# One granule's x transposed on SyncE's DMA queue instead of TensorE, its FFN half moved, and two granules' loads released later

## The chip, the cores and the metric

The kernel runs on one core of a Trainium2 chip. The metric is the device time of one execution in microseconds. Of the 47 executions of the kernel before that were timed beside the experiments, 46 lie within 0.3% of their median, 208.63 us (one took 209.83). "PE" is TensorE, "DVE" VectorE, "ACT" ScalarE, "POOL" GpSimd, "SP" SyncE. The profile's span is about 1.8 us shorter than the device time of the same execution (207.4 against 209.15 before, 212.9 against 214.69 changed).

## The reference

```python
# attention: q, k, v are (4 batches, 8 heads, 768 positions, 64), float32
scores = q @ k.T / sqrt(64) + bias(head, distance)
keep   = (key position < 8) | (0 <= row - column < 96)
x = (softmax(where(keep, scores, -1e9)) @ v)      # -> (3072 tokens, 512)
# feed-forward (FFN), with w_in (512, 2048), w_out (2048, 512)
h = x @ w_in
out = (s * relu(h)**2 + b) @ w_out                # (3072, 512) float32
```

## The kernel before

The 3072 tokens are handled as 12 granules of 256 tokens (numbers 0 to 11; three per batch). A granule passes through five stations:

1. GpSimd issues six loads (k, q and v of two blocks of 128 rows), cast to bfloat16 on the way.
2. k and q are transposed, by PE for granules 0 to 3, by four DMA transposes on SyncE's queue for the others.
3. PE makes scores, ACT the exponentials, DVE the masks, PE the product with v, DVE the normalised result `xn`.
4. `xn` is transposed to `xT`, by PE for granules 0 to 3 and by two DMA transposes on SyncE's queue for the others.
5. PE multiplies with `w_in` in eight pieces of 8 matmuls each (the first FFN half, 1.75 us for two pieces), ACT and DVE square, PE multiplies with `w_out`.

Loads are held back by a tiny copy on GpSimd that reads one element of something; everything behind it on the queue waits until that element is there (in the kernel before the gate of granule 8 waited 11.86 us, and the first load behind it was issued at 83.87 us, 0.40 us after it).

```python
X_PE, LEAD = 4, 4

def x_by_dma(j):
    t = xT_tile(j)
    for i in range(GB):                                    # two blocks
        nc.sync.dma_start_transpose(t[:, :, i * P : (i + 1) * P], xn[j][:, i, :])

def hold_loads(ap):                                        # the gate
    g = work.tile([P, 1], BF16, name="gate", tag="gate")
    nc.gpsimd.tensor_copy(g[0:1, :], ap)

def finish_granule(j):
    if j < X_PE:
        x_by_pe(j)
    else:
        x_by_dma(j)
    if 6 <= j + LEAD < NJ:                                 # loads of granule j + 4
        hold_loads(xT[j][0:1, 0, GT - 1 : GT])
        load_granule(j + LEAD)

def step(s, c0, c1, c2, pool=None, pre=()):                # half a granule, from granule 4 on
    j = 2 * s // HP
    last = (2 * s + 2) % HP == 0
    if not last and j >= 4 and j + 2 < NJ:
        qk_by_dma(j + 2)                                   # SyncE: k, q of granule j + 2
    posts = scores(s + 1)
    # ... exponentials, masks, c0, product with v, c1, product with v, c2 ...
    if last:
        finish_granule(j)
    # ...

# ... granules 0 to 3 by hand ...
finish_granule(3)
run(scores(8))
# ...
step(8, [lambda: rest(2, 0)] + late_p1(3, (0,)), late_p1(3, (1, 2)), late_p1(3, (3,)))
step(9, p2[2][1:2], late_p1(3, (4, 5)), late_p1(3, (6, 7)))
```

`late_p1(3, ...)` are pieces of the first FFN half of granule 3; `rest(2, ...)` and `p2[2]` are the output product of granule 2. SyncE's queue carries, in program order, the transposes of k and q, the transposes of x and the output stores. A transpose whose source has not landed stops all that is behind it (in the changed kernel's trace the queue stood 5.5 us for one k load of granule 6). "Landing" is the time when a transfer's data have arrived; where a landing time of two transposes is given, it counts from the issue of the second.

The softmax here doesn't subtract the row's maximum and nothing guards it: scores larger than these inputs give would overflow.

## Time and profile before

The median was 208.58 us in three runs (208.42 to 208.96).

| Reading | Before |
|---|---|
| PE busy | 202.1 of 207.4 us |
| longest wait of PE after the start | 0.51 us, for q of granule 5 |
| DMA engines | busy nearly without a pause from 40 to 79 us |
| PE transposes of granule 3's x | 0.54 us of PE time |

From the page of the kernel before: the span, the busy times, and two of the rows that cut the span into 40 slices (busy share in tenths).

```profile
span 207.4 us, 5323 instructions
...
PE 202.1 (97%) x2191; PEld 160.1 (77%) x2191; DVE 161.3 (78%) x338; ACT 128.5 (62%) x198; POOL 68.9 (33%) x90
...
PE   7999999999999999999999999999999999999993
...
DMA  5999999999999999999999999999570300240006
```

PE is busy all the time, so only PE work removed, or a wait of PE removed, can shorten the kernel. The DMA row: until about 140 us the DMA engines have hardly a free moment.

From PE's timeline of the kernel before (start, length, instruction group; in brackets the idle time before it and what ended it): the transposes that the change removes, the next scores, the one wait, scores, and the first FFN half of granule 5.

```profile
58.52 0.61 PE L591 MATMUL ps_x<-ident_bf,xn 128*128 128x128 bf16 x8
59.06 0.45 PE L441 MATMUL ps_s<-qx,kx 64*128 64x128 bf16 x8
...
69.10 0.34 PE L441 MATMUL ps_s<-qx,kx 64*128 64x128 bf16 x6 [0.51 <-DMA qx<-nat]
...
94.12 0.62 PE L441 MATMUL ps_s<-qx,kx 64*128 64x128 bf16 x16
...
98.35 1.91 PE L619 MATMUL ps<-xT,w_in_bf 128*128 128x256 bf16 x16
```

From POOL's timeline of the kernel before: the gates before the loads of granules 6, 7, 8 and 9.

```profile
51.16 0.18 POOL L122 COPY gate<-xT 1x1 bf16<-1x1 bf16 x1
...
61.62 0.18 POOL L122 COPY gate<-xT 1x1 bf16<-1x1 bf16 x1
...
83.29 0.18 POOL L122 COPY gate<-xT 1x1 bf16<-1x1 bf16 x1 [11.86 <-DMA xT<-xn]
...
97.71 0.18 POOL L122 COPY gate<-xT 1x1 bf16<-1x1 bf16 x1 [8.60 <-DMA xT<-xn]
```

From the DMA view of the kernel before, short windows around 60.2 and 91.2 us (last number: us from issue to landing): the last q transpose of granule 5 and the x of granule 5.

```profile
qx<-nat SPq DMA_TRANSPOSE x1, 8.9
...
xT<-xn SPq DMA_TRANSPOSE x2, 6.4
```

The x of granule 5 was issued at 89.92 and 91.23, and landed at 97.59. PE used it at 98.35.

### The profile page before, as it was taken

The numbers are of one execution on the slowest core, as the hardware profiler recorded it, in microseconds if no ns is written. First come the engines' busy times: TensorE is split into PE (matmuls) and PEld (weight loads), VectorE is DVE, ScalarE is ACT, GpSimd is POOL, SyncE is SP. The second block draws the span as 40 slices with busy tenths as digits, with TensorE's granted clock in tenths as the row PEclk, the third lists the DMA queues.
The fourth block names the chain that finished last, engine by engine and source line by source line (L and its number), as shares of the span: only waits on it lengthen the run. The fifth ranks groups of instructions, "written<-read, shape, count | busy, mean of one in ns | idle before, by whom it ended". The sixth has DMA issues, their size and how long they took to land.

```text
span 207.4 us, 5323 instructions
## 1 busy us (share of the span) xinstructions
PE 202.1 (97%) x2191; PEld 160.1 (77%) x2191; DVE 161.3 (78%) x338; ACT 128.5 (62%) x198; POOL 68.9 (33%) x90
## 2 busy tenths in 40 slices
PE   7999999999999999999999999999999999999993
PEld 2678884557867485878888898888888889888883
DVE  7786599977989856799799974699866696737974
ACT  5875669486976548786664595663695764476200
POOL 8985333799365300810900828200000000000000
PEclk9999999999999999999999999999999999999999
DMA  5999999999999999999999999999570300240006
GB/s 164 172 179 202 207 206 177 155 152 129 110 150 120 151 132 218 155 213 212 152 198 153 125 154 178 194 172 126 52 206 0 95 14 0 56 150 0 0 9 196
DMA packets 110836, 28.17 MB, mean 136 GB/s; under 512 B 97852, under 2 KB 109308, under 8 KB 110812
## 3 DMA queue, kind: packets, MB, share of 16 engines
q0 software_dynamic: 76000, 13.11, 90.1%
q1 hardware_dynamic: 33612, 14.13, 41.7%
q10 hardware_dynamic: 1200, 0.59, 1.1%
q8 instruction: 17, 0.28, 0.6%
q14 instruction: 7, 0.06, 0.1%
HBM read 27.26 MB, written 6.29 MB: 162 GB/s over the span
## 4 chain that ended last, share of the span: by engine, by line
PE 65%; DMA 23%; POOL 9%; issue 1%; DVE 0%; POOLq 0%
PE ps L619 29%; PE ps L819 24%; DMA nat<-in_q_dram 12%; DMA w_in_bf<-in_moe_w_in_dram 6%; PE ps L667 5%; DMA qx<-nat 4%; PE ps_s L441 4%; PE ps_av L495 3%; POOL vb L108 3%; POOL nat L102 3%; POOL w_in_bf L140 2%; POOL nat L116 1%; PE ps_last L819 0%; DVE o_last L828 0%; POOL rel L173 0%
## 5 line engine op out<-in xcount | busy, mean ns | idle before, releaser
L619 PE MATMUL ps<-xT,w_in_bf 128*128 128x256 bf16 x768 | 90.3, 273 | 0.0
L629 ACT ACTIVATE gT<-ps 128x512 bf16<-128x512 f32 x96 | 55.8, 599 | 46.8 <-PE ps L619 46.6
L619 PEld LDWEIGHTS <-w_in_bf 128*128 128x128 bf16 x768 | 73.0, 98 | 9.4 <-DVE xT L594 0.2
L450 ACT ACTIVATE pt<-ps_s 128x1024 bf16<-128x1024 f32 (+1 forms) x44 | 39.3, 946 | 3.3 <-PE ps_s L441 3.3
L667 PE MATMUL ps<-w_out_bf,gT 128*128 128x512 bf16 x128 | 29.7, 380 | 0.0
L457 DVE TENSOR_TENSOR pt<-pt,tmpl 128x1024 bf16<-128x1024 bf16 (+1 forms) x40 | 24.6, 645 | 3.8 <-ACT pt L450 3.7
L819 PEld LDWEIGHTS <-gsum 128*128 128x128 bf16 x256 | 24.1, 98 | 3.7 <-DVE gsum L782 0.5
L108 POOL DMA_DIRECT2D vb<-in_v_dram x24 | 21.4, 906 | 6.9 <-DMA w_out_bf<-in_moe_w_out_dram 3.4
L793 DVE TENSOR_TENSOR gT<-gT 128x1024 bf16<-128x1024 bf16 x20 | 13.7, 686 | 11.7 <-ACT gT L629 11.7
L667 PEld LDWEIGHTS <-gT 128*128 128x128 bf16 x128 | 11.7, 98 | 13.0
L466 DVE TENSOR_TENSOR xn<-ps_av,rc 128x256 bf16<-128x256 f32 x48 | 20.4, 425 | 1.7
L819 PEld LDWEIGHTS <-gT 128*128 128x128 bf16 x200 | 18.6, 98 | 2.3
L465 DVE RECIPROCAL rc<-ps_av 128x4 f32<-128x4 f32 x48 | 8.6, 179 | 12.3 <-PE ps_av L495 10.4
L116 POOL DMA_DIRECT2D nat<-in_k_dram x16 | 14.2, 885 | 9.2 <-DMA nat<-in_k_dram 5.1
L495 PEld LDWEIGHTS <-pt 128*128 128x128 bf16 x320 | 14.4, 97 | 2.7 <-DVE xn L466 0.7
L632 DVE TENSOR_TENSOR gT<-gT 128x512 bf16<-128x512 bf16 x32 | 13.0, 422 | 3.5 <-ACT gT L629 3.3
L495 PE MATMUL ps_av<-vb,pt 128*128 128x65 bf16 x208 | 15.5, 193 | 0.0
L819 PE MATMUL ps<-w_out_bf,gsum 128*128 128x256 bf16 x128 | 15.3, 273 | 0.0
L116 POOL DMA_DIRECT2D nat<-in_q_dram x16 | 14.2, 888 | 2.9 <-DMA w_in_bf<-in_moe_w_in_dram 1.9
L819 PE MATMUL ps<-wsub,gsum 128*128 128x256 bf16 x128 | 15.1, 273 | 0.0
L819 PE MATMUL ps<-w_out_bf,gT 128*128 128x256 bf16 x120 | 13.9, 273 | 0.0
L122 POOL COPY gate<-xT 1x1 bf16<-1x1 bf16 x6 | 1.1, 176 | 35.9 <-DMA xT<-xn 35.9
(112 smaller groups left out, 228.5 us busy)
## 6 DMA issues: line engine op xcount, KB each, us to landing
out_dram<-o_q SPq DMA_DIRECT2D x15, 256.0 KB, 2.6
vb<-in_v_dram POOLq DMA_DIRECT2D x24, 128.0 KB, 8.3
nat<-in_k_dram POOLq DMA_DIRECT2D x22, 128.0 KB, 7.7
nat<-in_q_dram POOLq DMA_DIRECT2D x22, 128.0 KB, 7.6
w_out_bf<-in_moe_w_out_dram POOLq DMA_DIRECT2D x4, 512.0 KB, 16.2
w_in_bf<-in_moe_w_in_dram POOLq DMA_DIRECT2D x4, 256.0 KB, 7.4
w_in_bf<-in_moe_w_in_dram POOLq DMA_DIRECT2D x2, 512.0 KB, 11.3
out_dram<-o_sb SPq DMA_DIRECT2D x4, 256.0 KB, 6.3
```

Source lines behind the costliest of these rows:

```text
L108: nc.gpsimd.dma_start(vbuf[b % 2][:, sb, :, 0:D], rows_of(v, b, sb))
L116: nc.gpsimd.dma_start(t[:, n, i, :, :], rows_of(srcs[n], b, sb))
L450: nc.scalar.activation(pt[:, :, 0:ncol], ps[:, :, 0:ncol], ACT.Exp, scale=QSCALE)
L457: nc.vector.tensor_tensor(pv, pv, m.rearrange("p h a c -> p h (a c)"), ALU.mult)
L466: nc.vector.tensor_tensor(dst, av[:, :, :, 0:D], rc[:].to_broadcast((P, 2, 2, D)), ALU.mult)
L495: nc.tensor.matmul(av[:, i, hi, 0 : D + 1], lhsT=pt[:, hi, c * P : (c + 1) * P], rhs=vv, start=(n == 0), stop=(n == len(terms) - 1),)
L619: nc.tensor.matmul(ps[:, i, :], lhsT=w_in_bf[:, kc, fc * P : (fc + 1) * P], rhs=xT[j][:, kc, :], start=(kc == 0), stop=(kc == KC - 1),)
L629: nc.scalar.activation(gs, ps[:], ACT.Relu)
L632: nc.vector.tensor_tensor(gs, gs, gs, ALU.mult)
L667: nc.tensor.matmul(po[:], lhsT=g_of(j)[:, fc, tb * P : (tb + 1) * P], rhs=w_out_bf[:, fc, :], start=(fc == 0), stop=(fc == FC - 1),)
L793: outs.append(lambda: nc.vector.tensor_tensor(gs, gs, gs, ALU.mult))
L819: nc.tensor.matmul(ps[:, tb, cs], lhsT=stat[:, fc, tb * P : (tb + 1) * P], rhs=mov[:, fc, cs], start=(fc == 0), stop=(fc == NH - 1),)
```

## The change

The intent: take granule 3's eight transposes and two copies off PE, DVE and ACT; give its x time to arrive by putting granule 2's output product first; and keep loads out of the way of the transposes, by releasing granule 6's loads when granule 3's x has landed and granule 7's when the q transposes of granule 6 have landed.

```diff
-    X_PE = 4
+    X_PE = 3
...
-        if 6 <= j + LEAD < NJ:
+        if 8 <= j + LEAD < NJ:
             hold_loads(xT[j][0:1, 0, GT - 1 : GT])
             load_granule(j + LEAD)
...
             qk_by_dma(j + 2)
+            if j == 4:
+                hold_loads(qk_of(2, 1)[0:1, 1, HP - 1, P - 1 : P])
+                load_granule(7)
...
     finish_granule(3)
+    hold_loads(xT[3][0:1, 0, GT - 1 : GT])
+    load_granule(6)
...
-    step(8, [lambda: rest(2, 0)] + late_p1(3, (0,)), late_p1(3, (1, 2)), late_p1(3, (3,)))
-    step(9, p2[2][1:2], late_p1(3, (4, 5)), late_p1(3, (6, 7)))
+    step(8, [lambda: rest(2, 0)], [lambda: p2_mm(2, 1, 0, FC // 2)], [lambda: rest(2, 1)])
+    step(9, late_p1(3, (0, 1, 2)), late_p1(3, (3, 4)), late_p1(3, (5, 6, 7)))
```

## The prediction

> **What bounds the kernel now.** PE. The page gives it 202.1 of 207.4 us busy, at a granted clock of 0.998. After the start its timeline shows one wait over 0.2 us: 0.51 us at 68.6, the scores of granule 5, "<-DMA qx<-nat". So the change can gain only removed PE work plus that wait, and loses any new PE wait.
>
> From 40 to 79 us the DMA engines hardly rest (stretches: DMA share 1.7 to 2.8). Transposes and loads slow each other: those of granule 5 took 8.4 to 8.9 us from issue to landing (the last 60.19 to 69.06), against 2.4 to 2.5 us with no load in flight (147 us, 163 us). [...]
>
> **What changes.** Gone: eight PE transposes of x (58.52 to 59.06, 0.54 us of PE), a 0.42 us DVE and a 0.58 us ACT copy. Added: two DMA transposes (1.2 to 1.3 us of SyncE's issue each). Moved: four FFN pieces of granule 3 behind granule 2's output; loads of granules 6 and 7 start later.
>
> **Critical path.**
> 1. The 0.54 us is mostly not kept there: granule 4's last transpose lands at 59.12, its scores start at 59.06 now. From 58.5 PE would wait about 0.5 us.
> 2. Granule 5's loads are queued before granule 6's, so still land at about 60.2; its transposes then run nearly alone and land at 64 to 66, not 69: the 0.51 us wait goes. Granule 3's x, issued behind them at 61.7 to 64.3, lands at 66 to 68; PE wants it at about 68.8. Thin margin, no wait.
> 3. Granule 6's loads start at about 67.5 instead of 51.3, 7's at about 80 instead of 61.7: a serial chain of loads (first landing 4.2 us, six issues 5.3 us), transposes, loads, transposes, 12 to 13 us a round. Granule 6 is ready at 79 to 81 (wanted 81.2), 7 at 92.5 to 95 (wanted 93.6).
> 4. Granule 7's transposes, waiting for loads until about 89, head SyncE's queue before output stores and granule 5's x. That x, now issued at 89.92 and landed at 97.59, would land at 99 to 100; PE wants it at 98. I expect 0.5 to 1.5 us of new PE wait there or at granule 7's scores.
>
> Sum: 208.58 - 0.5 + about 0.7 = 208.8 us, 80% range 207.7 to 210.6. Faster by over 2%: 0.01 (there are not 4 us to take). Within 2%: 0.95. Slower by over 2%: 0.04.
>
> **What would show each step.** PE's timeline: a wait near 58.6 for granule 4's qx, none near 68.5; granule 5's transposes landing in 4 to 6 us; GpSimd's gate copies at 66 to 68 and 79 to 81; PE waits for "qx<-nat" near 94 or "xT<-xn" near 98; PE busy down about 0.5 us.
>
> **What would make it wrong.** If rounds take 10 us, step 4's waits vanish: 207.9 to 208.1. If 15 us, waits of 2 to 4 us appear at granules 6 and 7: 211 to 213. If granule 5's loads land earlier, everything after shifts earlier. PE could wait for PSUM where all eight FFN pieces of granule 3 now stand together (ACT 0.60 us each beside two exponentials of 0.97, against PE's 0.87 each); I expect it not to.

## The result

The changed kernel took 215.28 us (median of four runs, 214.69 to 216.16) against 208.50 (208.34 to 208.96). The ratio is 1.0325, 95% interval 1.0285 to 1.0365. Ratios here are the mean time of one kernel's fast runs over that of the other's fast runs of the same rounds, so they are not quite the ratio of the medians. On this one core a run is called slow when it is over 1.5% above the fastest run of the same kernel; the medians below are over all runs.

From the page of the changed kernel:

```profile
span 212.9 us, 5299 instructions
...
PE 202.5 (95%) x2175; PEld 160.4 (75%) x2183; DVE 161.2 (76%) x337; ACT 127.9 (60%) x197; POOL 69.9 (33%) x90
...
PE   6999999999999999975899999999999999999993
...
DMA  5999999999996999999999999994161210240005
```

PE's row has a hole that was not there before, in the slices 18 to 20 counted from the left (90 to 106 us). In the DMA row the first breath comes in slice 13, at 64 to 69 us, where the held loads had only just been released (65.14 us) and had not landed.

From PE's timeline of the changed kernel:

```profile
58.77 0.40 PE L441 MATMUL ps_s<-qx,kx 64*128 64x128 bf16 x8
...
93.20 0.23 PE L441 MATMUL ps_s<-qx,kx 64*128 64x128 bf16 x2
94.53 0.57 PE L441 MATMUL ps_s<-qx,kx 64*128 64x128 bf16 x14 [1.10 <-DMA qx<-nat]
...
102.00 2.73 PE L619 MATMUL ps<-xT,w_in_bf 128*128 128x256 bf16 x16 [3.12 <-DMA xT<-xn]
104.87 2.63 PE L619 MATMUL ps<-xT,w_in_bf 128*128 128x256 bf16 x16
```

Up to 93 us the change works. The first wait is gone, and PE starts the scores of granule 7 at 93.20 instead of 94.12, 0.92 us earlier. Then PE waits 1.10 us for the q of granule 7 and 3.12 us for the x of granule 5. After that the same 16 matmuls take 2.73 and 2.63 us that took 1.91 before.

From POOL's timeline of the changed kernel, the gates before the loads of granules 6, 7, 8 and 9:

```profile
65.14 0.18 POOL L122 COPY gate<-xT 1x1 bf16<-1x1 bf16 x1 [14.10 <-DMA xT<-xn]
...
78.19 0.40 POOL L122 COPY gate<-qx 1x1 bf16<-1x1 bf16 x1 [7.32 <-DMA qx<-nat]
...
83.90 0.32 POOL L122 COPY gate<-xT 1x1 bf16<-1x1 bf16 x1
...
102.08 0.18 POOL L122 COPY gate<-xT 1x1 bf16<-1x1 bf16 x1 [12.66 <-DMA xT<-xn]
```

Granule 6's loads start 14 us later than before, granule 7's 16.6 us later, granule 8's 0.6 us later. So the loads of 7 and 8, whose issues had 12.4 us of rest between them (71.4 to 83.9), now follow each other without a pause from 78.7 to 89.4 us. The last load of granule 8 landed at 97.13 before and lands at 104.43 now.

From the DMA view of the changed kernel, short windows around 59.5, 62.6 and 92.6 us: the last q transpose of granule 5, the x of granule 3, the x of granule 5.

```profile
qx<-nat SPq DMA_TRANSPOSE x1, 4.6
...
xT<-xn SPq DMA_TRANSPOSE x2, 2.5
...
xT<-xn SPq DMA_TRANSPOSE x2, 9.3
```

The q transpose, beside the last packets of granule 5's loads, lands in 4.6 us, and the x of granule 3, with no load packet from 62.5 to 65.1 us, in 2.5: the late release does what it was meant to do there. But the x of granule 5, issued at 91.35 and 92.62, lands at 101.95.

From the table by stretches of the changed kernel (busy us of each engine, then the granted clock, DMA share and GB/s):

```profile
core 0: us, PE busy (x) PEld busy (x) DVE busy (x) ACT busy (x) POOL busy (x), PEclk, DMA share, GB/s
102.00:104.00 2.00, 2.00 (x14) 1.61 (x15) 0.00 (x0) 0.60 (x1) 1.50 (x3) 0.74 1.30 233
104.00:106.00 2.00, 2.00 (x16) 1.49 (x15) 0.87 (x3) 0.60 (x1) 2.00 (x3) 0.50 1.54 223
```

The clock record of the trace has 0.5 from 102.94 on for 3.41 us. Half a clock for 3.41 us costs 1.7 us (an estimate). The same stretches of the kernel before ran at 1.00.

The balance of the two profiled spans: 0.92 us gained by 93 us, then 1.10 + 3.12 of waits and 1.7 of half clock lost; that makes +5.0, and the spans differ by 212.9 - 207.4 = 5.5 us. About half a microsecond is not put down to anything. The profiled execution of the changed kernel was its fastest; the other three had clocks of 0.983 to 0.991.

### The profile page after: what moved, and what is told of

The parts are those of the page before. It is cut to its first block, busy times and chain, and to the rows that moved or that the text cites. A ratio compares the mean times of both kernels' runs of the same rounds, so it can differ in the third digit from the quotient of the medians.

```text
span 212.9 us, 5299 instructions
## 1 busy us (share of the span) xinstructions
PE 202.5 (95%) x2175; PEld 160.4 (75%) x2183; DVE 161.2 (76%) x337; ACT 127.9 (60%) x197; POOL 69.9 (33%) x90
## 4 chain that ended last, share of the span: by engine, by line
PE 89%; DMA 7%; ACT 1%; issue 0%; SPq 0%; ACTq 0%; DVE 0%
PE ps L619 40%; PE ps L819 21%; PE ps L667 13%; PE ps_s L441 5%; PE ps_av L495 5%; DMA xT<-xn 4%; DMA first<-in_q_dram 3%; PE ps_t L351 1%; PE ps_s L517 1%; PE ps_s L532 1%; PE ps_av L558 1%; PE ps_x L591 0%; PE ps_t L341 0%; PE ps_last L819 0%; SPq L599 0%
## 5 line engine op out<-in xcount | busy, mean ns | idle before, releaser
L619 PE MATMUL ps<-xT,w_in_bf 128*128 128x256 bf16 x768 | 91.5, 275 | 3.2 <-DMA xT<-xn 3.1
L667 PE MATMUL ps<-w_out_bf,gT 128*128 128x512 bf16 x120 | 28.7, 379 | 0.5 <-issue 0.2
L793 DVE TENSOR_TENSOR gT<-gT 128x1024 bf16<-128x1024 bf16 x20 | 13.7, 686 | 12.4 <-ACT gT L629 12.4
```

The source lines that it names most:

```text
L619: nc.tensor.matmul(ps[:, i, :], lhsT=w_in_bf[:, kc, fc * P : (fc + 1) * P], rhs=xT[j][:, kc, :], start=(kc == 0), stop=(kc == KC - 1),)
L667: nc.tensor.matmul(po[:], lhsT=g_of(j)[:, fc, tb * P : (tb + 1) * P], rhs=w_out_bf[:, fc, :], start=(fc == 0), stop=(fc == FC - 1),)
L793: outs.append(lambda: nc.vector.tensor_tensor(gs, gs, gs, ALU.mult))
```

## The experiments

Theory A: granule 7's loads come late, so its transposes block SyncE's queue late; granule 5's x is issued late behind them and shares the DMA engines with granule 8's loads; PE waits, and the idle time brings the half clock. Rival B: the loss comes of granule 3's x on SyncE's queue, or of PE's new order. All kernels below gave correct results. "Before" was run again beside each batch (medians 208.54 to 208.90).

| Run | Median us | Ratio to before (95%) | PE waits over 0.5 us after 60 us, in its profile |
|---|---|---|---|
| changed kernel | 215.28 | 1.0325 (1.0285 to 1.0365) | 1.10 (q of 7), 3.12 (x of 5) |
| late_loads | 213.57 | 1.024 (1.0193 to 1.0286) | 2.95 (x of 5) |
| queue_order | 211.41 | 1.0133 (1.0097 to 1.0169) | 2.45 (x of 3) |
| order_only | 208.86 | 1.0007 (0.9993 to 1.002) | none |
| x5_pe | 210.66 | 1.0095 (1.006 to 1.0131) | 0.96 (q of 7), 0.99 (x of 6) |
| busy_wait | 213.46 | 1.0257 (1.0195 to 1.0319) | 1.40 (q of 7) |
| hold8 | 212.94 | 1.0177 (1.0117 to 1.0237) | 1.31 (x of 5), 1.24 (q of 8) |
| pool_stores | 211.60 | 1.0127 (1.0104 to 1.015) | 2.69 (q of 7) |
| defer | 212.97 | 1.0229 (1.017 to 1.0287) | 2.08 (q of 7) |
| hold8_act | 214.30 | 1.0248 (1.0209 to 1.0287) | 1.92 and 2.75 (ACT) |
| hold8_defer | 217.12 | 1.0386 (1.0332 to 1.044) | 1.67 and 3.88 (q of 8) |
| seven_free | 213.30 | 1.0212 (1.0189 to 1.0236) | 1.09 (q of 6), 2.27 (x of 4) |
| seven_nat6 | 216.40 | 1.0186 (1.0162 to 1.021), two fast runs | 3.62 (x of 4) |
| seven_nat6_x4 | 213.40 | no interval, one fast run | 2.67 (x of 5) |
| queue_six_nat5 | 209.30 | 1.0033 (1.0019 to 1.0048) | 0.83 (x of 3) |
| split5 | 210.57 | 1.0096 (1.0063 to 1.0129) | 2.13 (q of 5) |
| six_nat5, six_nat5b | 208.68, 208.78 | 0.9996 (0.9983 to 1.001), one run | none |

### Which part of the change loses: late_loads, queue_order, order_only

late_loads is the kernel before with only the gates moved. As granule 3's x is made by PE there, the first gate reads the last q transpose of granule 5, which opens at nearly the same time (64.26 against 65.14 us).

```diff
# late_loads, against the kernel before
-        if 6 <= j + LEAD < NJ:
+        if 8 <= j + LEAD < NJ:
...
+            if j == 4:
+                hold_loads(qk_of(2, 1)[0:1, 1, HP - 1, P - 1 : P])
+                load_granule(7)
...
     finish_granule(3)
+    hold_loads(qk_of(1, 1)[0:1, 5, HP - 1, P - 1 : P])
+    load_granule(6)
```

> The kernel before with only the loads moved: granule 6's released by the landed q transposes of granule 5, granule 7's by the landed q transposes of granule 6; granule 3's x stays on PE and PE's order is the old one. Theory A (the loss is the serial chain of late loads: granule 7's transposes late, granule 5's x late, PE waits, clock drops): gates open at about 64 and 77 us, PE waits for qx near 94 and for xT near 98 as in the changed kernel, time 212 to 215. Rival B (the loss comes of granule 3's x on SyncE's queue or of the new PE order): 208 to 209, no wait over 1 us near 98.

PE's timeline of late_loads near 100 us:

```profile
100.99 3.55 PE L619 MATMUL ps<-xT,w_in_bf 128*128 128x256 bf16 x16 [2.95 <-DMA xT<-xn]
```

213.57 us: the late loads alone cost 4.8 of the 6.8 us, with the wait for granule 5's x at the same place, and a stretch of 3.41 us at half clock behind it (100.95 us on). The other wait that was expected, for a q near 94, did not come. Rival B cannot explain this, as granule 3's x is on PE and PE's order is the old one. Theory A is only half right, though. The DMA view of late_loads, a window around 91.2 us, has for granule 5's x:

```profile
xT<-xn SPq DMA_TRANSPOSE x2, 9.7
```

Its two transposes were issued at 89.99 and 91.27 here, as in the kernel before (89.92 and 91.23), and landed at 100.94 instead of 97.59. So here nothing was issued late, and the whole delay lies between issue and landing.

queue_order is the complement: the changed kernel with the old gates. order_only also sets `X_PE` back to 4.

```diff
# queue_order, against the changed kernel (order_only: and X_PE = 4)
-        if 8 <= j + LEAD < NJ:
+        if 6 <= j + LEAD < NJ:
...
-            if j == 4:
-                hold_loads(qk_of(2, 1)[0:1, 1, HP - 1, P - 1 : P])
-                load_granule(7)
...
-    hold_loads(xT[3][0:1, 0, GT - 1 : GT])
-    load_granule(6)
```

> The changed kernel with the loads of granules 6 and 7 released as in the kernel before (granule 2's x, granule 3's x): the queue and order part of the change alone. Theory A (the late loads carry the loss): granule 3's x and the q transposes of granule 5 share the DMA engines with granule 6's loads again and land at about 69 and 71, PE waits 1.5 to 3 us near 69, no wait near 94 or 98, time 208.5 to 210.5. Rival B (queue and order carry the loss): 213 or more.

PE's timeline of queue_order near 70 us:

```profile
71.69 4.15 PE L619 MATMUL ps<-xT,w_in_bf 128*128 128x256 bf16 x24 [2.45 <-DMA xT<-xn]
```

Here granule 3's x shares the DMA engines with granule 6's loads, takes 8.8 us to land, and PE waits 2.45 us. This may be why the change moved the gates at all. The time, 211.41, is above the 208.5 to 210.5 that was expected; the wait lies in the range expected, and two of six runs (213.1 us) had a clock of 0.991 and 0.992; the profiled one of the two had the half clock.

> The kernel before with only PE's new order (granule 2's output ahead of all eight FFN pieces of granule 3), x of granule 3 on PE, loads as before. Theory A: nothing changes, 208 to 208.9, the wait of about 0.5 us for the q transposes of granule 5 near 68 stays. Rival B2 (eight FFN pieces in one step wait for PSUM): 1 us or more longer, with waits of PE between 69 and 77.

208.86 us against 208.90: PE's new order costs nothing, and eight FFN pieces in a row do not run out of PSUM here (no PE wait over 0.5 us after 60 us in its profile). The wait of 0.5 us that I expected to stay was not in its profile.

### The half clock: busy_wait

28 matmuls that nobody reads were put before the FFN piece that waits.

```diff
# busy_wait, against the changed kernel (step 13)
+    def fill(n, w=2 * P):
+        ps = ps_h.tile([P, w], F32, name="ps_w", tag="psh")
+        for _ in range(n):
+            nc.tensor.matmul(ps[:], lhsT=ones_bf[:], rhs=w_out_bf[:, 0, 0:w], start=True, stop=True)
...
-            [u1(o, 0)],
+            [lambda: fill(28)] * (pr == 2) + [u1(o, 0)],
```

> The changed kernel with 28 matmuls of 256 columns that nobody reads (about 3.05 us) put before the FFN piece that waits for granule 5's x, so that PE works through the wait. If the half-clock stretch is caused by the idle time, it vanishes and the time falls by 1.4 to 1.7 us to about 213.5, with the FFN piece starting at the same time. If the clock drop has another cause, the time stays at 215.

PE's timeline and the table by stretches of busy_wait:

```profile
98.84 3.22 PE L1169 MATMUL ps_w<-w_out_bf,ones_bf 128*128 128x256 bf16 x28
101.99 1.91 PE L619 MATMUL ps<-xT,w_in_bf 128*128 128x256 bf16 x16
...
102.00:106.00 4.00, 4.00 (x49) 3.44 (x50) 1.21 (x3) 1.93 (x4) 3.58 (x5) 1.00 1.44 222
```

The FFN piece starts at 101.99, as in the changed kernel (102.00), but its 16 matmuls take 1.91 us and the clock is 1.00. The median falls to 213.46, as expected. Here doing nothing useful is faster than waiting: the half clock is a consequence of the idle time, and it makes a wait of 3.1 us cost 4.8 (an estimate: 3.1 + 1.7). The medians fall by 1.8 us and the profiled spans by 1.6 (212.9 to 211.3); the intervals of the two ratios overlap a little, and one run of four still took 216.05 us at a clock of 0.992, so the size rests on the profile, the cause on both.

The clock records say more (worked out from them and from PE's timelines). In the changed kernel's record 98.99 us at full clock is 29 times 3.413 us, then come 3.41 at half, then 105.81 at full clock, 31 times; in the record of the kernel before the 201.39 us at full clock are 59 times. So in these two records the clock changes at whole steps of 3.413 us. The idle time of PE within the 3.41 us that end where a half clock begins was 1.85 us in queue_order, 2.08 in defer, 2.47 in the changed kernel, 2.56 in pool_stores, 2.62 in hold8_act, 2.67 in seven_nat6_x4, 2.92 in late_loads and 3.18 in hold8_defer. A longer wait of 3.62 us in seven_nat6 was followed by no half clock, nor was one of 2.27 in seven_free or one of 2.13 in split5. Steps of 3.413 us cut these waits into 1.93 and 1.69, 0.94 and 1.33, 1.02 and 1.11 (an estimate from the clock records and the PE timelines). So the length of a wait does not settle alone whether a half clock follows. That it matters where among the steps a wait falls is my reading of these numbers; no run moves a wait along them to test this, and 1.85 us within one step was followed by a half clock while 1.93 was not.

### What makes granule 5's x late: x5_pe, hold8, pool_stores, defer, hold8_act, hold8_defer

```diff
# x5_pe, against the changed kernel
-        if j < X_PE:
+        if j < X_PE or j == 5:
             x_by_pe(j)
```

> The changed kernel with granule 5's x transposed by PE. Theory A with the clock drop as a second-order loss: the wait of 3.1 us for xT and the stretch of 3.4 us at half clock vanish, 0.54 us of PE work comes back, the wait of 1.1 us for qx stays: 5.5 - 3.1 - 1.7 + 0.5 = 1 to 1.5 us over before in the span, 209.5 to 211. Rival C (granule 5's x is only the first thing that is late, the next ones stop PE as long): over 213.

210.66 us. The wait and the half clock went, the wait for granule 7's q stayed, as theory A has it. PE's timeline of x5_pe holds one more wait than expected:

```profile
95.48 0.57 PE L441 MATMUL ps_s<-qx,kx 64*128 64x128 bf16 x14 [0.96 <-DMA qx<-nat]
...
117.53 1.92 PE L619 MATMUL ps<-xT,w_in_bf 128*128 128x256 bf16 x16 [0.99 <-DMA xT<-xn]
```

With granule 5's x out of the way, granule 6's x is the next that comes late.

hold8 moves granule 8's loads away from granule 5's x.

```diff
# hold8, against the changed kernel
-        if 8 <= j + LEAD < NJ:
+        if 9 <= j + LEAD < NJ:
...
                 load_granule(7)
+            if j == 5:
+                hold_loads(qk_of(2, 1)[0:1, 3, HP - 1, P - 1 : P])
+                load_granule(8)
```

> The changed kernel with granule 8's loads released by the landed q transposes of granule 7 instead of granule 4's x. Theory A1 (granule 5's x is late because granule 8's loads share the DMA engines with it; in the changed kernel its transposes took 9.3 us from issue to landing against 6.4 before): it lands in 4 to 6 us, at about 97, waits near 94 and 98 shrink to under 0.5 us together, time 207.5 to 209. Theory A2 (it is late because it is issued late, behind granule 7's transposes on SyncE's queue): issue stays at 91.4, landing at 99 or later, wait over 1 us, time over 210. Granule 8 itself may come late near 108.

PE's timeline of hold8:

```profile
98.75 1.92 PE L619 MATMUL ps<-xT,w_in_bf 128*128 128x256 bf16 x16 [1.31 <-DMA xT<-xn]
...
110.54 0.57 PE L441 MATMUL ps_s<-qx,kx 64*128 64x128 bf16 x14 [1.24 <-DMA qx<-nat]
```

From POOL's timeline of hold8, the gate and the first load behind it:

```profile
91.74 0.18 POOL L122 COPY gate<-qx 1x1 bf16<-1x1 bf16 x1 [8.05 <-DMA qx<-nat]
92.31 0.88 POOL L116 DMA_DIRECT2D nat<-in_k_dram  x1 [0.40 <-DMA out_dram<-o_sb]
```

The x, issued at 90.82 and 92.45, landed 6.2 us after issue instead of 9.3, at 98.7. The gate opened while its transposes were being issued, and packets of the loads run from 94 us on, so hold8 delays the sharing with granule 8's loads and does not take it away: the 3 us are a part of what the sharing costs. I had expected 97 and waits under 0.5 us together; x still came 1.3 us late, and granule 8's q now came late too. 212.94 us, with a wide spread (211.1 to 213.8 in fast runs).

The rest is the place in SyncE's queue, behind output stores. In the changed kernel the last input of granule 5's x was ready at 87.8 us. Its transposes were issued at 91.35, because granule 7's transposes (until 88.8) and four of the five output stores stood ahead. pool_stores issues the five stores from GpSimd; defer issues them on SyncE behind the x.

```diff
# pool_stores (defer: the same five, appended to a list that is issued after x_by_dma(5))
-        nc.sync.dma_start(out[t0 : t0 + P, :], o_sb[:])
+        nc.gpsimd.dma_start(out[t0 : t0 + P, :], o_sb[:])
```

> The changed kernel with five output stores (granule 3's first block, the four early ones) issued from GpSimd instead of SyncE, so that granule 5's x is not behind them: in the changed kernel its last input was ready at 87.8 and its transposes were issued at 91.35. Head of line theory: issue at 88.9 (after granule 7's transposes), landing at 97 to 99.5, the wait at x falls from 3.1 to under 1.5 us, the half clock goes, time 210 to 212. Contention theory: issued earlier but landing not before 101, time stays at 214 to 216.

> The changed kernel with the same five output stores issued on SyncE after granule 5's x instead of before it. Head of line alone: x issued at 88.9 to 90.5 instead of 91.35, landing at 97.5 to 100 beside granule 8's loads, wait at x 0.5 to 2 us (changed kernel 3.1), the wait of 1.1 us at granule 7's q stays; 210.5 to 213.

PE's timeline of pool_stores (first line) and of defer (second line):

```profile
96.45 0.93 PE L441 MATMUL ps_s<-qx,kx 64*128 64x128 bf16 x14 [2.69 <-DMA qx<-nat]
...
96.11 0.67 PE L441 MATMUL ps_s<-qx,kx 64*128 64x128 bf16 x14 [2.08 <-DMA qx<-nat]
```

In both the x's first transpose was issued about 1.3 us earlier, at 89.99 and 90.11. The second landed 7.7 and 7.5 us after its own issue instead of 9.3, at 99.03 and 98.85. So of the 3 us gained, less than half is the earlier issue; the rest is a shorter time from issue to landing, as the four stores of 256 KB no longer stand in front. (In the changed kernel's trace SyncE's queue moves the stores' packets of 2 KB from 94 to 97 us, before the x's packets of 256 bytes.) PE no longer waited for the x of granule 5, beyond a short wait at 83 us (0.34 and 0.39 us) that is granule 4's. But in the same runs the wait for granule 7's q grew from 1.10 to 2.69 and 2.08 us, and the half clock, which was expected to go, followed that wait instead (3.41 us from 96.32 and from 96.44). 211.60 and 212.97 us: both in their expected range, though not by the split of waits that I expected.

hold8_act and hold8_defer move both the stores and granule 8's loads away from the x.

> hold8 with the five output stores issued from ScalarE, so that granule 5's x is neither behind them on SyncE's queue nor beside granule 8's loads. If these two together are why it is late: issued at about 89, landing at 94 to 96, PE waits for no x near 98 (hold8: 1.3 us, changed kernel: 3.1 us), half clock gone. What is left is granule 8 itself (1.2 us near 110 in hold8): time 208.5 to 210.5. If a wait over 1 us at x stays, a third cause is at work.

This one is spoilt. The x's first transpose landed after 4.0 us and no wait for x was left, but ScalarE now stood still at the stores: it had been idle for 3.69 us before 82.32 us, with a store issued at 81.89 (the trace names DVE as what it waited for), and for 3.42 us before 94.00, with two stores issued from 92.63 on (the trace names a q transpose). PE waited 1.92 and 2.75 us for ACT. Its time says nothing about the theory.

> Both taken away without ScalarE's queue, which spoilt hold8_act: granule 8's loads held until granule 7's q has landed, and the five stores behind granule 5's x on SyncE. If these two are the whole cause of the late x: it lands at 93.5 to 96, no wait at 98 and none at granule 7's q, no half clock; left is a wait of 1 to 2 us for granule 8's q near 110: 208.5 to 210.5.

From the DMA view of hold8_defer, a window around 90.3 us, and from its PE timeline:

```profile
xT<-xn SPq DMA_TRANSPOSE x1, 2.5
```

```profile
109.67 0.23 PE L441 MATMUL ps_s<-qx,kx 64*128 64x128 bf16 x2 [1.67 <-DMA qx<-nat]
113.78 0.93 PE L441 MATMUL ps_s<-qx,kx 64*128 64x128 bf16 x14 [3.88 <-DMA qx<-nat]
```

The x was issued at 89.07 and landed at 92.76, over 9 us before the changed kernel's, and PE waited neither for it nor for granule 7's q. Granule 8's loads were issued from 91.64 and have no packets before 93 us, so here the x was on its way almost alone. The stores ahead of it in the queue and granule 8's loads beside it are together the whole cause of the late x. Yet the kernel took 217.12 us, the slowest of all. Granule 8's loads, held back, now ran into granule 9's, released at 96.84: PE waited 5.55 us in two waits for granule 8's q, and the clock was at half for 6.83 us. The expected 208.5 to 210.5 was wrong: I priced what the hold removed and not what it pushed forward.

### Releasing granule 7 earlier: seven_free, seven_nat6, seven_nat6_x4

```diff
# seven_free, against the changed kernel: loads of 7 right behind those of 6
-            if j == 4:
-                hold_loads(qk_of(2, 1)[0:1, 1, HP - 1, P - 1 : P])
-                load_granule(7)
...
     load_granule(6)
+    load_granule(7)
# seven_nat6: loads of 7 released by landed loads of 6
-                hold_loads(qk_of(2, 1)[0:1, 1, HP - 1, P - 1 : P])
+                hold_loads(nat[6][0:1, 1, 1, H - 1, D - 1 : D])
# seven_nat6_x4: and granule 4's x by PE
```

> The changed kernel without the second gate: granule 7's loads follow granule 6's at once at about 71. If the second turn of the chain is what costs, granule 7 is ready by 88, granule 5's x is issued at 89 to 90 and lands by 97, the waits at 94 and 98 and the half clock vanish: 207.5 to 208.6. Risk: granule 6's transposes share with granule 7's loads and land at 80 to 81.5 (wanted 80.8), a wait of up to 1 us there.

> The changed kernel with granule 7's loads released by the landed loads of granule 6's q (about 74) instead of by its landed transposes (78.2): 4 us earlier, while granule 6's transposes still run mostly beside granule 6's v loads. Expected: granule 6 in time, granule 7 ready at 89 to 91, granule 5's x lands at 97 to 98.5, waits there under 0.8 us together, no half clock, 207.6 to 208.8.

> As seven_nat6 with granule 4's x on PE. The wait of 3.6 us for that x goes, 0.54 us of PE work comes back; granule 8's loads follow granule 7's at once (80 to 86) and are through before granule 5's x is issued at about 89: it lands at 95 to 97, no wait. 207.9 to 209.5. If granule 7's transposes are delayed by granule 8's loads behind them and block SyncE's queue again, x of granule 5 waits and the time is 210 or more.

All three expectations failed in the same way. (seven_nat6_x4 had named 210 us or more for the case of a blocked queue; but the x of granule 5 was issued at 89.74, as hoped, and its landing was late.) PE's timeline of seven_nat6:

```profile
86.66 1.91 PE L619 MATMUL ps<-xT,w_in_bf 128*128 128x256 bf16 x16 [3.62 <-DMA xT<-xn]
```

Granule 7's loads now met the x of granule 4 (landing 7.6 us after issue in seven_free and 7.8 in seven_nat6, 2.5 in the changed kernel, where they had not started). With granule 4's x on PE, granule 8's loads opened at 80.75 and the x of granule 5 took 10.0 us and came 2.67 us late. Each release hits another transpose that PE needs at once.

seven_nat6 also shows what "slow" may mean on one core. Two of its six runs took 212.3 and 212.8 us at a clock of 1.0; four took 216.0 to 217.4 at 0.981 to 0.984 and were called slow, being over 1.5% above the fastest. The profiled run is one of the first two. It had an idle stretch of 3.62 us and no half clock. In the four others the lower clock is on record, but no profile of mine shows where. The ratio of the two fast runs therefore leaves out a loss that may belong to the kernel; the same holds for seven_nat6_x4, with one fast run of six (209.83 us), and for one run of hold8.

### Looking for a version that beats both: queue_six_nat5, split5, six_nat5

Granule 6's loads can be released between the two extremes, by the landed loads of granule 5 (about 60 us). six_nat5 does only this to the kernel before; queue_six_nat5 adds the change's queue and order; split5 also issues granule 3's x between the two blocks of granule 5's transposes.

```diff
# six_nat5, against the kernel before; queue_six_nat5, against queue_order
-            hold_loads(xT[j][0:1, 0, GT - 1 : GT])
+            if j == 2:
+                hold_loads(nat[5][0:1, 1, 1, H - 1, D - 1 : D])
+            else:
+                hold_loads(xT[j][0:1, 0, GT - 1 : GT])
# split5: and
-    qk_by_dma(5)
+    qk_by_dma(5, [0])
...
             x_by_dma(j)
+        if j == 3:
+            qk_by_dma(5, [1])
```

> The kernel before with one gate moved: granule 6's loads wait for granule 5's landed q loads (about 60) instead of granule 2's x (51.2). Granule 5's transposes then share less, the wait of 0.5 us near 68.6 goes, granule 6 and 7 land at most 1 to 2 us later than before: 207.7 to 208.6. If granule 4's x (before: landed 0.7 us before PE wanted it) is hit by granule 7's loads: 209 to 211.

> The changed kernel's queue and order, granule 6's loads released by granule 5's landed q loads (about 60), granule 7's by granule 3's landed x as in the old gates. Granule 3's x lands at 67 to 69.5 instead of 71.6 (old gates) or 65.1 (changed kernel), PE wants it at 68.6: wait 0 to 1 us. Granule 7's loads at about 68 to 74 then meet granule 4's x: landing 82 to 85, wanted 83, wait 0 to 2 us. Time 208 to 211.

> queue_six_nat5 with granule 3's x issued between the two blocks of granule 5's transposes, at about 58.5 instead of 61.5, because the second block waits for its loads until 59.5. Expected: x lands at 63 to 66, the wait of 0.8 us for it goes, granule 5's q lands at 66 to 68 (wanted 68), time 207.8 to 208.6. If it only trades one wait for the other: 209 to 209.6.

> six_nat5 again for a profile, because the profiled execution of the first ran at half speed throughout. Expected: no wait at granule 5's scores near 68.5, granule 5's transposes landing in 5 to 7 us, otherwise the waits of the kernel before; span 206.5 to 207.5.

queue_six_nat5, 209.30 us, is the best form of the change: 0.33% slower than before instead of 3.25%. Its x of granule 3 still comes 0.83 us late. split5 repaired that wait and got another of 2.13 us at granule 5's q, as its loads of granule 7 were released by the earlier x at 65.7 instead of 69.8 us and shared with it (7.5 us to landing). six_nat5 ties with the kernel before (ratio 0.9996). six_nat5b, its second look, shows no PE wait over 0.15 us after 60 us and a span of 207.0 us. So the 0.51 us wait of the first profile could be removed without a gain that five rounds can see. order_only had no such wait either and was no faster. The profiled execution of the kernel before took 209.15 us, longer than all of its other runs in the first rounds, so its wait may not have been in the others; no run decides it. None of the versions beats the kernel before.

## Why the prediction was wrong

- "What bounds the kernel now": right. PE was the limit, and everything lost is PE idle or PE at half clock.
- Step 1, a wait of 0.5 us for granule 4's q near 58.6: it did not come. That q landed at 58.50 in the changed kernel and not at 59.12, and the scores started at 58.77, 0.29 us earlier than before. With the old gates it also came at 58.48 (order_only) and 58.72 (queue_order), with held loads at 59.55 (six_nat5b), so the step rested on one value of a time that scatters.
- Step 2, granule 5's transposes land at 64 to 66 and granule 3's x at 66 to 68: right and a little pessimistic (64.11 and 65.08). No wait there.
- Step 3, gates at about 67.5 and 80, 12 to 13 us a round: right in form and size (65.14, then 13.05 us to 78.19). Granule 6 came in time, granule 7's q 1.10 us late.
- Step 4 named the right mechanism and the right place, but the term was mis-sized. I wrote "would land at 99 to 100" for granule 5's x and "0.5 to 1.5 us of new PE wait". Landing was at 101.95, the wait there 3.12 us, and the wait at granule 7's q was another 1.10: 4.2 us together. The issue of its second transpose was about where I had it: 92.62, against 92.6 to 93.6 (99 to 100 less the 6.4 us that the kernel before took from issue to landing). What I got wrong was the time from issue to landing. I had carried over about 6.4 us, though I had myself moved granule 7's loads right in front of granule 8's; it took 9.3 us. So of the 4.4 us by which the x landed later than before, 1.4 is later issue and 3.0 is a longer way from issue to landing. late_loads shows the longer way with no later issue (9.7 us), and hold8_defer shows 2.5 us without granule 8's loads and the stores. I wrote "or" between two waits that both came.
- The term left out: the half clock, 1.7 us. I listed the wait but not what a wait of 3 us can do to the clock. busy_wait shows this term by itself.
- Sum: with 4.2 and 1.7 in place of 0.7, the same sum gives 208.58 - 0.5 + 5.9 = 214.0 us; measured were 214.69 in the profiled run and a median of 215.28.
- "If 15 us, waits of 2 to 4 us" named the size of the loss as a case of failure, but for the wrong reason: the round took 13 us.
- The worry about PSUM was rightly put aside (order_only).

The change itself loses because it delays 12 loads by about 15 us in a stretch where the DMA engines had no slack. The eight transposes taken off PE were worth 0.54 us. queue_order and late_loads lose 1.3% and 2.4% each alone, and the changed kernel 3.25%. In its profile the late loads have removed the wait of queue_order (x of granule 3), and a wait for granule 7's q has come that late_loads does not have; whether the two parts simply add up the intervals do not decide.

## What to carry to other kernels

Before you hold back loads to make room for a transfer that is needed soon, list what those loads will meet when they are released, and read the landing times of that stretch under the new traffic, not under the old one. In the stretch here, where the DMA engines were full, a delayed load was only moved onto the next just-in-time transfer: the releases tried here put PE waits of 0.8 to 5.6 us on the q of granules 5 to 8 and the x of granules 3 to 6, and only six_nat5 put none. A PE wait of about 2 us or more should be priced with the stretch at half clock that can follow it (here 1.7 us on top of 3.1; waits of 2.08 us and more were followed by it in eight profiles; waits of 2.13, 2.27 and 3.62 us were not), and a margin of 0.8 us in front of a transfer on a busy queue was no margin (that transfer, the x of granule 5, came 4.4 us later).

## What the runs show of the clock, the queue and one slow execution

- Idle stretches of PE of 2.08 us (defer), 2.45 (queue_order), 2.95 (late_loads) and 3.12 us (changed kernel) were each followed by 3.41 us at 0.5, while one of 3.62 us (seven_nat6) was not. Within the 3.41 us before the half clock 1.85 us of idle time was enough in queue_order; the 3.62 us of seven_nat6 put at most 1.93 us into one such step (an estimate, see busy_wait), and no half clock followed. So no single length of one idle stretch, read from these runs, is a safe allowance.
- Two blocks of 128x512 bfloat16 took, from the issue of the second transpose to its landing, 2.5 us alone (hold8_defer), 6.4 in the kernel before, 7.5 and 7.7 beside granule 8's loads (defer, pool_stores), 9.3 with four output stores ahead as well (changed kernel), and 10.0 in seven_nat6_x4.
- One run of six_nat5 out of six took 415.39 us (span 413.6), correct, with PE busy for 407.7 us instead of 202.1, the FFN matmuls at a mean of 443 ns instead of 273, the activations of ACT unchanged (597 ns against 599), and no clock record in its trace. The five others took 208.3 to 208.7. So PE alone took about twice its time, from end to end; no run shows why.
